# A recurrence with mixture-of-experts attention on one core: a newly searched order, 33 warming products, alternating quarters

## The chip, the cores and the metric

The kernel runs on one core of a Trainium2 chip. The time is the device time of one execution in microseconds; the number to compare is the median of several executions. Engines: TensorE (PE) multiplies matrices, VectorE (DVE) and ScalarE (ACT) work element by element and read PE's results, GpSimd (POOL) works element by element on the main on-chip memory alone, SyncE (SP) issues the loads and stores.

## What is computed

Two stages, in float32. The first is a recurrence over 768 time steps for 4 batches and 8 heads of width 48:

```python
for t in range(S):
    cur = einsum('bhd,bhe->bhde', u * k[t], v[t])
    y[t] = einsum('bhd,bhde->bhe', r[t], state + cur)
    state = w[t][:, None] * state + einsum('bhd,bhe->bhde', k[t], v[t])
```

Its output x, 4 x 768 x 384, goes into causal attention with 4 experts, of which each token uses the 2 with the largest gate:

```python
logits = x @ w_gate                       # top 2 of 4, softmax of the two
for e in range(4):
    q, k, v = x @ wq[e], x @ wk[e], x @ wv[e]         # width 64
    a = softmax(causal(q @ k.T / 8))
    out += gate[e] * (a @ v @ wo[e])
```

## The kernel before

The work is cut into 8 units: 4 batches, each in two halves of 384 steps. Every unit runs first a recurrence part, then an attention part. The recurrence part takes the 8 heads as 4 pairs; a pair's 384 steps form 6 chunks of 64. For each pair, VectorE and GpSimd build running products of the decay by scans (`w`, `suf`, lines 518 to 524), scale the streams `lt` with them (527, 529), and form `kt` (531) and `pre` (533, called `mr` in the planner). PE transposes `kt` (`ktp`), ScalarE evicts that (`kts`), PE forms the chunk states `ups` (403), and VectorE chains them chunk by chunk into `wst` (414); the first chunk of a pair is only copied (ScalarE or VectorE). `ys` is `wst` scaled (424). PE forms the products inside a chunk, `aps` (585), for two pairs together; they are masked into `am` (590) and, with `ys`, give the output `yps` (356, 358). In unit one only, the bonus term u is a small product `rk` (509) and is added to `yps` by a product with the identity (363). In the other units it is done by VectorE, GpSimd and ScalarE (538 to 561).

The attention part transposes x (`xp`, `xh`, `xl`), projects it (`pp` for q and k, `vp` for v), and runs score tiles `sp` (787), their maximum on VectorE (798), the exponential on ScalarE (803), transposes `tp` (232, or 228 as whole blocks), products with v `yp` (845), the gates, and the output projection `op` (913).

The order on every engine is written out. Each piece of work is registered with `plan.add` under a kind, with the engines that may do it and an estimated duration. A table of numbers, `ORDER`, then lists all pieces in one order, each with a letter for its engine (P, V, A, G, S) and its number; `Plan.order` walks through it, and every engine executes its pieces in that order. Numbers that the list leaves out are not executed; a transpose becomes a whole-block one where PE's last product used the whole array. Two more rules come from the last loop of the kernel: a load on SP waits for the PE piece that stands ahead of it in the list ("pace"), and some GpSimd kinds wait for the last VectorE piece of certain kinds ahead of them ("port").

Numbers 5 to 98 are 94 possible warming products: multiplications of a block of zeros (line 965) whose result nobody reads. The list before executes 14 of them.

The estimated durations that the change touches are `T_SC` and `T_SC3` (score tiles by size) and the one of `aps`. They reach the chip only through the search that made the list.

Of the kernel before, what the change touches and what calls it, by code (L numbers as in the profile page):

```python
# [1012 lines left out]
P174 V255 P166 P212 V246 A175 V256 A167 A213 S352 P185 A186 S237 P229 A230 P187 A188 V258 V214 V189 G260 V215 V190 V216
S251 V191 V217 V192 G296 V218 A209 G219 S290 G194 V257 P26 V307 A184 V247 V292 P220 V221 G311 V223 G360 A248 V193 V293
V308 V259 V294 V312 V295 V313 P1127 V309 P1131 P225 A226 P227 V298 A228 P231 A232 V261 V355 P265 V300 A267 V262 V301 P233
V310 S252 S367 A266 A234 P281 P268 V282 V275 P319 V269 G297 V276 A249 S305 A284 V270 G314 V277 V271 V278 G299 V272 V279
A263 G280 V273 P1132 V302 V103 V356 V101 V370 V357 V359 V374 S408 A321 V358 V315 A264 S473 G274 V371 S368 P1128 G316 P1129
P1070 P1066 P1067 A320 P1068 A1130 P1133 G416 A1069 A303 P1071 P1072 A1134 P322 A1073 V329 A105 G285 V323 V330 V324 S306 A317 V331
P335 P1097 V1098 G411 P1074 V325 V332 V1100 V326 V333 V336 S409 G378 G415 V327 G379 P1075 V338 P1076 A1101 P1106 P286 S291 G362
V1078 G375 A318 A1099 G334 V1079 V1107 S353 V1109 V372 A1108 A1077 P1115 V287 A380 V288 V1116 P1104 A1105 A1117 V1118 P1086 P1111 A1112  # L1020
P1080 P1087 V373 S369 A381 V376 V361 V106 V419 S423 G328 V412 V377 G420 P1088 P1081 A1119 P1082 P340 A1110 V342 A1090 P1122 A1123
P1120 P1113 V341 V1091 V1085 A1121 A1114 V363 P1102 A1103 P349 V1092 A350 S488 V364 G1093 G426 P346 S107 A347 A1089 V351 V348 V365
A1084 A1083 P400 P382 P343 P1124 P1125 P1126 G476 G430 S354 V401 A383 A384 V403 A1094 A344 V345 V427 V1095 V413 P385 A421 A386
G431 V387 A393 S474 P1135 V1138 P1144 A1165 V1145 P1195 V1136 V394 A366 V388 V389 G417 G1096 V1147 V395 P1191 P1196 V414 S424 V396
V390 G418 G432 V397 P1197 A1146 A1148 P1153 S410 P1151 V428 V391 V398 A1198 V1154 P1199 P1192 V1156 P1193 A1152 P1200 A1137 P1140 A108
P1149 A1194 A1150 S542 A1141 V429 V480 V484 G392 G399 P1222 V496 V477 A1155 V481 V434 V482 V491 G433 P1231 V478 A1157 P1205 P1201
G495 V1234 V1232 A422 V479 P1206 A1203 A1202 P1207 V1204 A1139 P438 V492 P1158 A440 A1159 V1210 A439 G485 V1167 V1223 A1233 A1235 P10
P1259 P1260 P1142 S527 A1224 V1143 G435 V1225 P456 V459 V493 P441 A449 S489 A442 V450 V457 V451 G1168 V443 A1208 A1209 A436 V444
P405 P1169 V1170 V445 G497 V452 P1261 G109 P1160 V446 V407 G549 A1262 V406 A1161 V453 G483 P1211 S425 P1212 V447 P1171 V454 V1172
V545 A437 A486 G455 A1173 S605 V494 V550 V530 P1213 V1216 G499 A1214 P1242 V1245 S544 V531 V1174 G487 G534 P503 A505 A504 A1215  # L1030
P1162 P1163 P1164 A1166 A1246 G448 S543 P1236 A1238 V1243 P1239 A1241 P1175 V1176 A1177 V532 V500 V498 V1217 V533 S590 P1263 P1264 V546
G612 A1237 G1178 G1218 A1240 P1265 P1250 A1252 A1251 A1244 A1266 V501 G598 P506 V513 S591 V507 V508 V514 V509 V547 P519 V520 A522
P461 V462 A1226 V510 V515 G593 V463 S475 V516 A502 G535 S528 V517 V511 P1187 P1267 P1229 V1270 V1268 V537 V551 A1230 V536 G512
G518 A1269 V608 P1179 V597 G523 P1180 S646 P1227 A1228 A1219 S490 A1181 P1276 V1277 P1247 A1248 V1279 A1249 V1220 A1278 V548 V594 V609
V601 G553 G599 V595 P1183 P1184 P1272 P1287 V1290 A1185 A1273 V1288 V538 V554 V596 G614 G552 P557 A1280 P1188 P1253 P467 G613 P470
V610 A559 A558 A1291 P464 A468 A465 V466 V469 P1254 A471 P1255 V472 A1289 A1189 V555 G649 P560 V561 V562 S661 V567 A556 V563
P524 V568 V569 G539 A1271 V564 G1221 P573 G653 V570 S529 G600 S592 V526 V565 V571 V574 V525 V576 G664 V1306 V669 G572 G566
V611 V602 P1335 A540 V650 V654 S606 V651 P1256 P1257 P1258 V616 A1304 P1274 A1275 V665 A541 S711 V617 P1292 V652 P620 V615 A1293
G1307 G668 V618 G714 P1284 A621 A1286 P1336 A622 V666 G655 A1294 S647 P1393 P1394 P1337 P1395 A1285 P623 A1338 V603 P578 S726 A631
A624 V625 V626 A1396 V1397 A619 V1339 V632 V627 V580 V633 G656 S648 V579 V628 V634 V635 A604 V629 V636 V667 P1281 P1330 P1308  # L1040
V1309 G637 A1283 V718 V670 A1282 V657 S712 V719 S662 G630 V729 G671 S765 P1331 P1332 P638 P584 A585 G658 P1295 A1297 A1296 A1333
V1334 V639 V586 A641 P1398 P1399 P587 A588 V589 V733 V672 V715 V730 V673 G642 P1400 P1298 P581 A582 V583 A1401 S780 S607 V674
V1402 P676 A678 A677 G722 P1363 V1364 A659 P1299 P1300 P679 A687 A680 G772 V688 V681 V689 A675 G734 V682 S727 V690 G720 A660
S1182 G735 V683 V1366 V716 G723 G783 P694 V695 P1310 V1311 A1365 V691 S766 P1301 P1302 P1303 A1305 V684 V697 P643 V645 P1314 V1315
V717 V787 S1186 V721 V692 A1316 P1481 P1368 A1369 G693 V644 G686 G768 P1482 P1483 V1485 V685 V1484 G788 A724 V1486 V731 G737 P1459
# [136 lines left out]
```

## Time and profile before

| | |
|---|---|
| median of 3 executions | 325.89 us (325.88, 330.29, 325.89) |
| the profiled execution | 329.57 us, span of its instructions 327.8 us |
| mean granted TensorE clock | 0.978 of full |
| busy: TensorE / VectorE / ScalarE / GpSimd | 311.1 / 275.6 / 237.0 / 144.3 us |

Times in the rows are in us from the first instruction of the profiled execution. A row of the timeline gives start, duration, engine, line, operation, tile written and tiles read, how many records are merged, and in brackets how long the engine stood idle ahead of it and what released it. A float32 product leaves two records. [...]

### The profile page before, as it was taken

What the parts mean: (1) busy time and instruction counts of PE and PEld (TensorE: products, weight loads), DVE (VectorE), ACT (ScalarE), POOL (GpSimd) and SP (SyncE); (2) the same over time, 40 slices, a digit from 0 to 9 for tenths busy, and PEclk for the clock granted to TensorE, in tenths of its full rate; (3) what the DMA queues carried; (4) which work ended last, traced back from release to release, by engine and by line L of the source; (5) the groups of instructions that cost most, each with busy time, mean ns of one, the idle gap of its engine ahead of it and who ended that gap; (6) DMA issues with size and microseconds to landing.
All of it is one profiled execution on the core that took longest, in us unless ns stands there. A gap on an engine that the chain in (4) does not pass through costs nothing.

```text
span 327.8 us, 13409 instructions
## 1 busy us (share of the span) xinstructions
PE 311.1 (95%) x5343; PEld 253.0 (77%) x5343; DVE 275.6 (84%) x876; ACT 237.0 (72%) x860; POOL 144.3 (44%) x277
## 2 busy tenths in 40 slices
PE   5899999999999988999799999999999999999995
PEld 2687757778877875899686987799888877978684
DVE  6897999999999998999778999989788755467852
ACT  3437799889989977687757887748868638477961
POOL 2055455668475665766447863466310100210320
PEclk9976999999999999999989999999999999999999
DMA  7989686754652975754418381441200001020012
GB/s 261 302 209 246 185 184 179 180 144 116 176 161 68 236 214 119 220 144 112 98 33 255 75 226 20 130 141 40 75 27 2 1 2 49 2 83 15 3 54 92
DMA packets 17758, 39.98 MB, mean 122 GB/s; under 512 B 2592, under 2 KB 10528, under 8 KB 17696
## 3 DMA queue, kind: packets, MB, share of 16 engines
q1 hardware_dynamic: 17696, 39.13, 43.5%
q8 instruction: 42, 0.69, 0.9%
q14 instruction: 20, 0.16, 0.2%
HBM read 34.40 MB, written 4.72 MB: 119 GB/s over the span
## 4 chain that ended last, share of the span: by engine, by line
PE 64%; DVE 21%; issue 6%; ACT 4%; DMA 3%; POOL 1%; SPq 1%; DVEq 0%; POOLq 0%; ACTq 0%
PE yp L845 10%; PE sp L787 9%; PE pp L682 9%; PE op L913 7%; PE vp L720 6%; PE tp L232 5%; PE ups L403 3%; PE yps L358 3%; DVE wst L414 3%; DVE a L798 3%; PE yps L356 2%; PE aps L585 2%; DVE w L524 2%; DMA lt<-in_wkr_dram 2%; DVE am L590 2%
## 5 line engine op out<-in xcount | busy, mean ns | idle before, releaser
L798 DVE CUSTOM_DVE_ANT_0 a<-sp,causal 128x128 f32<-128x128 f32 (+5 forms) x96 | 56.7, 618 | 19.3 <-PE sp L787 14.4
L803 ACT ACTIVATE a<-a,mx 128x128 f32<-128x128 f32 (+5 forms) x96 | 64.2, 670 | 8.9 <-DVE mx L798 8.9
L236 ACT COPY ATa<-tp 128x512 f32<-128x512 f32 (+3 forms) x75 | 35.4, 491 | 18.7 <-PE tp L232 13.6
L845 PE MATMUL yp<-ATa,v_sb 128*64 128x384 f32 (+2 forms) x240 | 36.9, 440 | 0.5 <-DVE Ql L696 0.4
L414 DVE SCALAR_TENSOR_TENSOR wst<-wst,suf,ups 112x48 f32<-112x48 f32 x160 | 34.3, 257 | 2.8 <-ACT wst L236 1.6
L682 PE MATMUL pp<-xh,wh_qk 128*128 128x384 f32 x84 | 31.3, 373 | 1.1 <-DVE Ql L696 1.0
L787 PE MATMUL sp<-K,Q 64*128 64x384 f32 (+4 forms) x160 | 31.0, 423 | 1.1 <-DVE xl L624 0.6
L559 ACT ACTIVATE xn<-nat,rk 128x48 f32<-128x48 f32 x120 | 29.0, 327 | 1.3 <-DVE rk L552 1.3
L682 PE MATMUL pp<-xh,wl_qk 128*128 128x384 f32 x84 | 28.5, 339 | 0.0
L682 PE MATMUL pp<-xl,wh_qk 128*128 128x384 f32 x84 | 28.2, 336 | 0.0
L358 PE MATMUL yps<-ys,pre 64*64 64x48 f32 (+1 forms) x704 | 25.8, 225 | 1.9 <-issue 1.7
L232 PEld LDWEIGHTS tp<-ident,a 64*128 64x128 f32 x530 | 22.0, 139 | 7.0 <-issue 1.6
L232 PE MATMUL tp<-ident,a 64*128 64x64 f32 x530 | 26.0, 228 | 0.7 <-ACT ATa L236 0.4
L356 PE MATMUL yps<-vy,am 64*64 64x48 f32 x768 | 26.3, 225 | 0.0
L845 PEld LDWEIGHTS yp<-ATa,v_sb 128*64 128x64 f32 x240 | 15.4, 139 | 14.0 <-issue 10.1
L358 PEld LDWEIGHTS yps<-ys,pre 64*64 64x64 f32 (+1 forms) x704 | 22.8, 138 | 4.0 <-issue 2.6
L533 POOL TENSOR_TENSOR pre<-lt,w 128x384 f32<-128x384 f32 x18 | 16.8, 936 | 17.6 <-DVE lt L529 5.6
L356 PEld LDWEIGHTS yps<-vy,am 64*64 64x64 f32 x768 | 23.8, 139 | 0.0
L550 ACT ACTIVATE nat<-nat 128x48 f32<-128x48 f32 x102 | 23.3, 237 | 0.3 <-POOL nat L542 0.3
L424 POOL TENSOR_TENSOR ys<-wst,suf 112x240 f32<-112x240 f32 (+1 forms) x28 | 21.7, 787 | 2.9 <-DVE wst L414 2.0
L787 PEld LDWEIGHTS sp<-K,Q 64*128 64x128 f32 x160 | 15.3, 188 | 8.4 <-issue 3.2
L902 POOL TENSOR_TENSOR yl<-yr,yh 128x384 fp32r<-128x384 f32 x9 | 9.0, 1009 | 26.8 <-ACT yh L901 26.7
(160 smaller groups left out, 927.1 us busy)
## 6 DMA issues: line engine op xcount, KB each, us to landing
lt<-in_wkr_dram SPq DMA_DIRECT2D x56, 218.6 KB, 4.1
nat<-in_nat_dram SPq DMA_DIRECT2D x28, 432.0 KB, 4.2
vy<-in_vY_dram SPq DMA_DIRECT2D x32, 144.0 KB, 3.2
out_dram<-ob SPq DMA_DIRECT2D x24, 192.0 KB, 2.0
lt<-in_wkr_dram SPq DMA_DIRECT2D x3, 583.0 KB, 6.3
w_qk<-in_wqk_dram SPq DMA_DIRECT2D x1, 768.0 KB, 8.6
nat<-in_nat_dram SPq DMA_DIRECT2D x4, 144.0 KB, 6.0
w_vg<-in_wvg_dram SPq DMA_DIRECT2D x1, 390.0 KB, 7.1
```

Source lines behind the costliest of these rows:

```text
L232: nc.tensor.transpose(o()[:, h * 512 + i * 64:h * 512 + i * 64 + 64], src[r], ident[r, r])
L236: nc.scalar.copy(o, i)
L356: nc.tensor.matmul(to, am()[k, c, :], vy()[k, c, :], start=zero and x == 0, stop=not first and i == 2 and x == len(group) - 1)
L358: nc.tensor.matmul(to, pre()[r, c, 0:C], ys()[r, c, :], start=i == x == 0, stop=False)
L414: nc.vector.scalar_tensor_tensor(new, ws[0:112, c0 + c - 1, :], sfv()[0:112, c, 0:1], upk()[0:112, o], op0=ALU.mult, op1=ALU.add)
L550: nc.scalar.activation(o, o, AF.Copy, accum_out=rk()[:, i, h:h + 1])
L559: nc.scalar.mul(xn()[:, i, (2 * p + h) * D:(2 * p + h + 1) * D], v()[:, i, h, :], rk()[:, i, h:h + 1])
L682: nc.tensor.matmul(pp()[:, 0:384], w[:, qk, k, cs], x()[:, k, :], start=(k == j == 0), stop=(k == j == 2))
L787: nc.tensor.matmul(spv(x)[:, h, :], q_()[p, t], flat(k_())[p, o], start=j == 0, stop=j == len(terms) - 1)
L798: nc.vector.tensor_tensor_reduce(out=a()[:, 0:n].rearrange("p (a n) -> p a n", a=np_), in0=spv(x), in1=causal[:, S - n:S].rearrange("p (a ...
L803: plan.add("exp", {"ACT": t_exp(n)}, lambda e, x=x, y=y, mx=mx, a=a: nc.scalar.activation(a()[:, 0:n], a()[:, 0:n], AF.Exp, bias=mx(), sca ...
L845: nc.tensor.matmul(yp()[e * 64:e * 64 + 64, lo:hi], v_sb[ep]()[:, j, e * 64:e * 64 + 64], at, start=(j == 0), stop=(j == nj - 1))
```

## The change

The order of all pieces is replaced: 2,059 entries become 2,080. Of the pieces that both lists have, 207 change their engine: VectorE loses `kt` 8 times (18 to 10), and gains `mr` (14 to 18), `rw` (16 to 19) and a few more; VectorE has 8 pieces fewer in all, ScalarE 10 more, GpSimd as many as before. 33 warming products are executed instead of 14. The two products `aps` of unit one are issued in another order: for each chunk, first both heads of one pair, then both heads of the other, so that two products that follow each other use different quarters of the array; in the other units that sequence is what it was. The estimates for score tiles rise, and the one for unit one's `aps` as well; these numbers are only read by the search.

```diff
             def amat(e, two=two, apss=apss):
                 for c in range(NH):
-                    for h in range(2):
-                        for x, (_, kt, pre, *_) in enumerate(two):
+                    for a in range(2):
+                        for z in range(2):
+                            h, x = (z, a) if first else (a, z)
+                            kt, pre = two[x][1:3]
                             nc.tensor.matmul(apss[x]()[half(h if first else h ^ x), c * C:(c + 1) * C], kt()[half(h), c, :], pre()[half(h), c, 0:C],
                                              start=True, stop=True)
-            plan.add("aps", {"PE": T_APS * (2 if first else 1)}, amat, [k for t in two for k in t[1:3]], [(apk, x) for x in range(2)], mode="Q", claim=[t[3] for t in two])
+            plan.add("aps", {"PE": 1800 if first else T_APS}, amat, [k for t in two for k in t[1:3]], [(apk, x) for x in range(2)], mode="Q", claim=[t[3] for t in two])
...
-S110 S111 V1 S3 V2 V117 V118 S136 V119 V114 V120 S113 V121 V122 S195 S138 V123 V142 V139 V124 S112 V147 P21 S170
...
+S110 V1 P32 S111 S136 V2 S3 S113 S170 P26 V117 P12 V118 V119 V114 P11 P18 V120 P9 P36 V122 P13 P21 P37
...
-T_SC = (239, 452, 666, 880, 1094, 1307)
-T_SC3 = (220, 370, 530, 690, 890, 1045)
+T_SC = (302, 515, 729, 943, 1157, 1370)
+T_SC3 = (362, 434, 603, 763, 978, 1133)
```

On PE, at the start of the program, the order before has five warming products and then unit one's first bonus product and transpose (line numbers after the change are 2 higher there):

```order
L965 MATMUL warm_170<-causal 128x512
L965 LDWEIGHTS causal
L965 MATMUL warm_181<-causal 128x512
L509 MATMUL rk_183<-u_t,nat_125 64x1 x12
L232 MATMUL ktp_200<-ident,kt_135 128x64 x6
L509 MATMUL rk_215<-u_t,nat_139 64x1 x12
```

and the changed kernel, where the first row here is the twentieth warming product:

```order
L967 MATMUL warm_200<-causal 128x512
L967 LDWEIGHTS causal
L967 MATMUL warm_202<-causal 128x512
L509 MATMUL rk_205<-u_t,nat_134 64x1 x12
L967 LDWEIGHTS causal
L967 MATMUL warm_218<-causal 128x512
...
L967 MATMUL warm_225<-causal 128x512
L228 MATMUL ktp_227<-ident,kt_174 128x128 x3
L509 MATMUL rk_242<-u_t,nat_159 64x1 x12
```

The first `rk` has moved behind 16 more warming products, four more stand between it and the transpose, and that transpose is now done in whole blocks.

On SP, the first loads before (`lt_66` in two parts is the first pair's streams, the other `lt` are the other pairs'):

```order
L245 DMA lt_66<-in_wkr_dram 128x398
L245 DMA lt_66<-in_wkr_dram 128x768
L959 DMA u_t<-in_uT_dram 128x8
L245 DMA lt_67<-in_wkr_dram 128x1166
L245 DMA vy_128<-in_vY_dram 128x288
L245 DMA lt_68<-in_wkr_dram 128x1166
L245 DMA vy_133<-in_vY_dram 128x288
L245 DMA nat_125<-in_nat_dram 128x288
L245 DMA lt_69<-in_wkr_dram 128x1166
```

and after:

```order
L245 DMA lt_66<-in_wkr_dram 128x398
L245 DMA lt_66<-in_wkr_dram 128x768
L245 DMA lt_67<-in_wkr_dram 128x1166
L961 DMA u_t<-in_uT_dram 128x8
L245 DMA vy_122<-in_vY_dram 128x288
L245 DMA lt_68<-in_wkr_dram 128x1166
L245 DMA vy_163<-in_vY_dram 128x288
L245 DMA nat_134<-in_nat_dram 128x288
L245 DMA lt_69<-in_wkr_dram 128x1166
```

The sequence is nearly the same, but the pairs behind the tiles have changed places, and in the list the second to sixth load now stand behind the first warming product, the seventh behind the 12th and the next five behind the 16th; before, the first eight stood ahead of all PE work.

On GpSimd, behind the constants, the order before:

```order
L529 TENSOR_TENSOR lt_68<-lt_68 128x192
L501 TENSOR_TENSOR nat_268<-lt_69 128x2x192
L518 TENSOR_TENSOR w_271<-lt_66 128x199
L527 TENSOR_TENSOR lt_69<-lt_69 128x192
L424 TENSOR_TENSOR ys_343<-wst_87,suf_148 112x240
```

and after:

```order
L531 TENSOR_TENSOR kt_315<-lt_69,suf_284 128x2x192
L533 TENSOR_TENSOR pre_321<-lt_68,w_182 128x2x192
L424 TENSOR_TENSOR ys_373<-wst_86,suf_131 112x240
L424 TENSOR_TENSOR ys_387<-wst_87,suf_176 112x240
L527 TENSOR_TENSOR lt_67<-lt_67 128x192
```

GpSimd now begins with a `kt` and a `pre` of unit one, both of which VectorE did before.

## Rows read from the trace of the kernel before

**Rows 1.** The page: busy us (share of the span) and records of each engine.

```profile
PE 311.1 (95%) x5343; PEld 253.0 (77%) x5343; DVE 275.6 (84%) x876; ACT 237.0 (72%) x860; POOL 144.3 (44%) x277
```

**Rows 2.** Busy time by stretch, us: length, PE, weight loads, VectorE, ScalarE, GpSimd.

```profile
core 0: us, PE busy (x) PEld busy (x) DVE busy (x) ACT busy (x) POOL busy (x), PEclk, DMA share, GB/s
0.00:20.00 20.00, 14.54 (x202) 9.83 (x206) 16.18 (x52) 7.07 (x24) 5.97 (x19) 1.00 0.91 267
20.00:31.00 11.00, 10.74 (x239) 9.74 (x240) 9.25 (x30) 6.57 (x26) 3.36 (x4) 0.54 0.92 226
31.00:45.00 14.00, 12.89 (x252) 8.59 (x250) 14.00 (x39) 11.64 (x56) 6.92 (x9) 1.00 0.80 203
45.00:140.00 95.00, 91.00 (x1903) 72.16 (x1902) 91.94 (x292) 80.26 (x322) 60.92 (x101) 1.00 0.62 165
140.00:200.00 60.00, 57.80 (x1017) 48.90 (x1019) 52.80 (x169) 45.58 (x165) 36.47 (x67) 0.97 0.49 130
200.00:328.00 128.00, 124.12 (x1742) 103.78 (x1742) 91.41 (x300) 85.84 (x273) 30.67 (x79) 1.00 0.14 46
```

**Rows 3.** Timeline of PE, 0 to 32 us.

```profile
1.42 2.31 PE L965 MATMUL warm<-causal 128*128 128x512 bf16 x5 [1.42 <-POOL causal L255]
5.64 1.44 PE L509 MATMUL rk<-u_t,nat 64*64 64x1 f32 x24 [1.91 <-DVE nat L501]
...
14.32 2.82 PE L585 MATMUL aps<-pre,kt 64*64 64x64 f32 x48
...
18.06 0.82 PE L965 MATMUL warm<-causal 128*128 128x512 bf16 x3
18.83 0.86 PE L509 MATMUL rk<-u_t,nat 64*64 64x1 f32 x24
...
27.87 2.65 PE L585 MATMUL aps<-pre,kt 64*64 64x64 f32 x48
30.44 1.56 PE L675 MATMUL pp<-xh,w_qk 128*128 128x384 f32 x4
```

**Rows 4.** Timeline of VectorE, 7 to 31 us.

```profile
7.53 0.37 DVE L518 TENSOR_TENSOR w<-lt 128x199 f32<-128x199 f32 x1 [0.47 <-DMA lt<-in_wkr_dram]
...
13.16 0.37 DVE L518 TENSOR_TENSOR w<-lt 128x199 f32<-128x199 f32 x1 [1.10 <-DMA lt<-in_wkr_dram]
...
14.19 0.54 DVE L533 TENSOR_TENSOR pre<-lt,w 128x384 f32<-128x384 f32 x1
...
19.96 0.95 DVE L533 TENSOR_TENSOR pre<-lt,w 128x384 f32<-128x384 f32 x1
...
27.71 1.49 DVE L414 SCALAR_TENSOR_TENSOR wst<-wst,suf,ups 112x48 f32<-112x48 f32 x8 [1.58 <-ACT wst L236]
...
30.55 1.02 DVE L590 TENSOR_TENSOR am<-aps,dec_mask 128x384 f32<-128x384 f32 x2 [0.17 <-PE aps L585]
```

**Rows 5.** Timeline of SP's queue: the first loads' issue.

```profile
0.74 0.85 SPq L245 DMA_DIRECT2D lt<-in_wkr_dram  x2
...
2.10 0.43 SPq L245 DMA_DIRECT2D lt<-in_wkr_dram  x1
```

**Rows 6.** Timeline of PE: an `aps` of a later unit, four quarters.

```profile
58.65 0.93 PE L585 MATMUL aps<-pre,kt 64*64 64x64 f32 x48
```

**Rows 7.** Timeline of PE at 162 us, and busy time by stretch behind it.

```profile
162.20 0.27 PE L358 MATMUL yps<-ys,pre 64*64 64x48 f32 x4 [1.69 <-issue]
...
163.00:166.00 3.00, 3.00 (x22) 1.73 (x21) 2.41 (x8) 0.34 (x2) 1.30 (x5) 0.54 0.02 5
```

**Rows 8.** Groups by line: `kt` on VectorE and on GpSimd.

```profile
L531 DVE TENSOR_TENSOR kt<-lt,suf 128x384 f32<-128x384 f32 x18 | 10.4, 590 | 0.0
L531 POOL TENSOR_TENSOR kt<-lt,suf 128x384 f32<-128x384 f32 x14 | 13.1, 939 | 7.9 <-DVE inv_pre L522 3.1 <-DVE pre L533 2.4 <-DVE w L524 1.3
```

More of the change, by code (lines that the diff above doesn't have):

```diff
@@ L1013 @@
[L1013 to L1045, printed above, removed]
@@ new lines @@
+V121 V124 P35 P5 V139 V142 S172 P33 P6 P28 P25 S112 V123 V143 V146 S195 S137 V144 V176 V173 S171 V145 S138 V148
+P7 V177 P19 P30 P24 P20 V180 P115 P22 S4 P10 P17 P15 P126 A127 V147 V181 V149 S250 V201 V178 P140 A116 P128
+P34 A0 P31 S104 V198 S235 P16 V202 V205 P151 A152 P8 A129 A141 P153 S236 V179 G207 P29 A154 V155 G183 V130 V156
+P161 P23 P27 A150 V131 V162 S99 P14 A105 V157 V132 V158 V133 G135 V159 S196 P210 V134 V182 V253 V206 G160 V254 V164
+V203 G242 V243 A125 V204 V238 V208 P185 A211 P166 S304 S197 A186 A167 P168 S289 P187 V246 A169 V239 P174 V247 A188 S290
@@ new lines @@
+V258 P229 A175 V189 V240 V190 P212 V213 A230 P220 V191 S306 G244 V214 V192 G257 V215 V193 V241 G194 V259 A184 V216 G245
+P199 V221 G296 V217 V223 S251 V255 A100 V218 V311 A248 A200 V256 V292 V307 V300 P1131 V293 P1127 G219 A209 P225 S352 V260
+V308 V294 P227 A249 V312 V297 V261 P265 V301 V262 V313 A226 V298 V355 V295 A228 A266 S367 A267 V359 V299 P231 P281 A232
+P268 V375 V269 V275 A284 V270 V302 P233 V276 S305 A234 V271 A102 G101 P1128 V277 V272 V282 V278 P1129 P1132 G285 V273 V309
+V279 A263 G274 V360 V370 V310 V371 V314 A264 G280 A303 V315 V356 V316 V357 P1066 S353 P1067 P1133 P1070 A1134 V374 V358 S252
@@ new lines @@
+P1071 P1072 A1073 P319 S237 A320 S423 A1130 A321 P1068 P1074 P1075 P322 P335 S368 V336 V329 A1069 P1097 A317 A338 V1098 V1100 P1076
+V330 G376 V323 V372 S408 V331 V324 V1079 A1099 A1077 G361 V332 P1080 V325 V326 G339 V333 V327 P1106 A1101 P286 S291 V1109 G363
+G334 A318 A1110 P1115 G328 V1107 A1078 S409 V103 P1081 P1113 V373 V378 V411 P1082 P1086 P1087 P1088 V1118 V1116 A1114 A1083 V287 V1085
+G377 V288 G364 S473 V1091 A1108 V362 V415 P1104 V379 V1092 G426 P340 A1117 A1119 V341 A1090 A1105 V342 P1102 V106 V416 S488 A1103
@@ new lines @@
+A1089 P1120 V412 V380 A1121 P1122 A1123 S107 P1111 A1112 P349 A350 V351 P382 G1093 S354 A383 P346 G431 A384 A347 P1124 V348 A365
+P400 G419 V401 P385 A393 A386 P343 V403 P1125 A1084 A1094 P1126 G480 P1135 A344 V394 A381 G476 S424 V345 V395 V1138 V1136 P1144
+V413 V396 V387 G417 V1147 V427 V414 V1095 P1153 V1145 A1137 V388 A1165 A1148 P1191 V1154 V428 A366 P1195 V389 A1146 P1192 P1140 A1141
+G481 G418 V1156 P1193 V397 P1196 V390 A1194 V398 A1155 S410 G1096 P1149 A1157 G399 P1151 P1199 P1197 A1198 V391 S369 V429 V491 A1152
@@ new lines @@
+A1150 V477 G392 V434 V420 V430 P1200 A1139 P1201 A1202 P1222 P1231 V492 A1203 V433 A421 V1204 A108 V1232 G432 S474 G495 V1234 V1167
+G482 V478 V435 V479 P1205 P1206 G1168 P1207 P1142 A1209 A1143 P1259 A1233 P1158 P438 V1223 A1159 V1210 S542 A440 G109 A439 G484 A422
+V1225 P1260 V436 P1261 G497 A1224 P456 P441 A442 S489 P405 V459 V457 A449 V443 A1208 V450 V444 A1262 V451 P1169 P1160 S527 A1235
+A1161 V1170 V407 P1211 V445 V406 A437 P1212 S543 V483 V452 P1171 P1213 V446 G485 V453 G545 V447 V454 A1215 S590 P1242 V1172 A1214
@@ new lines @@
+G499 V493 A1226 A1173 S544 S425 V1245 P1239 V1216 A1241 V1243 A1240 G1174 V530 V535 P1162 P1163 A1246 P1164 V496 A1166 V494 A486 V500
+G448 P1175 V498 V1217 P503 V531 P1236 G455 A504 V546 A1237 P1263 P1250 V549 A505 A1238 A1251 V532 V1176 P1264 P1265 P506 V501 A1252
+A1177 P519 V507 V513 G1218 V520 V514 V508 G598 P461 A1266 A522 V1178 V533 A1219 V509 S475 V515 V462 V510 V516 V511 V517 G593
+V463 G523 P1267 V1270 V1268 A502 G551 G534 V547 V553 G518 A487 V537 V550 S490 V536 S591 G597 P1179 S528 S605 G601 P1187 P1229
@@ new lines @@
+A1230 A1244 P1227 A1228 P1180 P1276 V1279 A1181 V1277 V554 S661 V1220 V548 P1188 V594 A1271 P1247 A1269 A1248 V538 V552 V539 A1249 G512
+P1183 A1280 G608 P1272 P1184 P1287 A1273 P557 G664 A1185 V1288 V1290 S646 G602 A1278 A559 A558 V595 V540 A1289 G612 G1221 P1253 V555
+P1254 G668 P467 A468 P470 A471 V469 P464 P1255 A465 V472 V466 V599 V609 P1256 A1189 A556 V596 G614 P560 V567 S606 P573 V561
+V610 V568 V574 P524 V569 V562 V570 G600 A576 S592 V563 G577 A603 V571 V525 G572 V526 P1335 V564 S529 V649 P1336 P620 A1291
@@ new lines @@
+A622 V611 S711 A621 V650 P1337 A1338 V1339 G613 V565 V1306 G616 V651 A604 P1257 P1258 P623 A631 A624 V632 A1304 V615 A541 S647
+G566 V617 V652 V665 G653 V625 V633 P1274 P1330 P1284 V626 A1286 S662 P1331 V634 P1393 S1182 P1332 P1394 A1285 G1307 A1275 A1333 P638
+V627 V635 V628 P578 G655 V1334 V636 G714 G657 P1308 G672 S648 A618 G630 V639 V629 P1395 V641 V580 V579 V1309 A619 S607 S726
+A1396 V1397 V654 P1281 A1283 A1282 P1295 A1297 A1296 V673 V670 G637 V715 P1292 G658 G669 V666 G719 A1293 P1398 P1310 V1311 A1294 P1363
@@ new lines @@
+P584 P587 A588 A585 P1399 P1314 V1366 P1400 V1364 A1312 A1367 V589 S712 V586 A1401 V667 V656 P581 A582 P676 A677 A678 V671 S780
+V583 V716 G729 A674 A659 V1402 G734 P643 P679 V680 P694 V730 A687 V733 V717 V681 V688 V731 G721 A697 G735 P1298 V689 V644
+P1299 S765 P1300 P1301 P1302 V645 S663 V695 V682 P1303 V718 V722 V732 V723 G736 A675 P1372 A1305 P1381 P1459 G720 P1460 V1315 V690
+P1481 V683 V691 S727 A660 S713 P1461 G787 P1482 V684 G698 V692 V685 G772 V1382 A1365 V1375 V1373 S766 S828 P1483 P741 A1462 A1316
@@ new lines @@
+A1485 V1463 V1484 P1368 V1486 P1529 P1469 V1384 P1530 G693 V768 V783 V788 V1313 V769 A1385 V737 A742 V770 P1470 P1531 P1471 G686 V738
+G1317 V724 P757 A1369 A743 P744 A1532 V1533 S843 A1473 V771 V745 A1374 V746 P699 A1472 G773 V1474 V751 V758 A725 A1383 G831 V752
+V753 S781 V747 V701 A739 P1475 P1534 P1476 P1477 A1478 V754 G775 A1479 P1535 G776 V700 V1480 V748 V784 V749 A1376 P1536 A1537 A760
+V785 P1464 G846 V1538 V755 V786 G756 P1370 V1487 P1465 G1488 P1466 P705 A1467 V1468 P702 P1326 S728 A706 V707 A703 P1327 V704 V740
@@ new lines @@
+V971 S965 P1672 A1673 P876 P825 V877 S901 G958 A826 P822 V879 A1563 V968 G1025 V827 A823 A1561 V824 V1674 P1523 P1524 P1525 P1526
+P1527 P1528 V1578 P1556 A1557 A1558 G1026 A1576 G973 P1553 G1579 V954 V955 A1555 S1325 G910 A1554 V969 P881 G975 V883 A898 P1564 A1566
+A1565 P1567 V970 A1568 P1455 P1736 G911 G1021 P1456 A1457 S886 V882 P1737 P1546 A1569 P1580 P1738 V1581 A1739 A1547 V912 P1582 V1583 V1740
+G974 P917 A918 A925 V919 V920 V926 V927 V921 G959 S966 G1006 V928 A1584 P932 V922 G976 S950 V923 V935 A977 V929 V930 G924
```

92 lines of the change are left out of this document (40 added, 52 removed).

## The prediction

> **What bounds the kernel now.** I read the share of busy time first, then busy time by stretch, then the waits of TensorE and VectorE in order of time. VectorE (DVE) is busy 84% of the span [rows 1], but by stretch [rows 2] the kernel has three parts. From 200 us on TensorE (PE) works 124.12 of 128 us and VectorE only 91.41: there PE's work alone sets the time. (From 140 to 200 us it works 57.80 of 60, and most of the rest is one wait, below.) From 45 to 140 us both are nearly full, PE 91.00 and VectorE 91.94 of 95 us, so either could be the limit and the slack is 4.0 us on PE and 3.1 us on VectorE. From 0 to 45 us VectorE is full from 31 on (14.00 of 14.00), and before it stands idle 3.8 us (0 to 20) and 1.75 us (20 to 31), while PE is idle 5.5 us in 0 to 20.
>
> The clock matters only at the start. The profile prints a granted clock of 1.00 for 0 to 20 us, but PE's own rows contradict it [rows 3]: the 24 records of `rk` at 5.64 us took 1.44 us, and the same 24 at 18.83 took 0.86; five warming products at 1.42 took 2.31 us (0.46 each), three at 18.06 took 0.82 (0.27 each). [...] Ahead of the first rise PE waited 1.42 and 1.91 us [rows 3]. [...]
>
> [...]
>
> **Which time the sum is made against.** The profiled execution took 329.57 us, the median run 325.89. The profiled one has one wait of 1.69 us inside `yps` at 162.20, released by nothing shown, and behind it the granted clock is 0.54 for 3 us [rows 7]; PE then loses about half of those 3 us. 1.7 + 1.5 = 3.2 us. The order of work does not ask for that wait, so a usual run is taken as 329.57 - 3.2 = 326.4 us, which is 0.5 above the median.
>
> **The change, part by part.**
>
> *Warming products*, 14 become 33, 21 of them ahead of the first `rk`. At 0.46 us each they end at 1.42 + 9.7 = 11.1 us, at 0.27 each at 7.1 us, so the first `rk` product moves from 5.64 to between 7 and 11 us. Behind it stand `ktp`, `ups`, and ScalarE's first `wst` copy, for which VectorE waits with its first `wst` step. That step has 28 VectorE instructions of unit one ahead of it before and 29 after, so it comes at the same 16 us; a PE that is 1.5 to 5.5 us late is covered by its 5.5 us of idle time. Without that cover every us would be paid. What they give: PE has no long gap ahead of 17 us, so its clock should rise early and hold. [...]
>
> *VectorE at the start.* Ahead of the second `aps` stand 13 fewer VectorE instructions (7 fewer `wst` steps, 2 fewer `kt`, `mr` and `pre` each); at the mean of a VectorE record, 275.6 / 876 = 0.31 us [rows 1], that is 4.1 us. So the second `aps` can go from 27.87 [rows 3] to about 24, and the first projection `pp` from 30.44 to about 26. But ahead of the last `yp` product of unit one's first two experts stand 6 more VectorE instructions than before (+1.9 us), ahead of the same place in unit three 2 fewer, ahead of the first `yp` of unit four 3 more (+0.9): the work is put in another order, not lowered, until PE alone is the limit. So the gain is in waits, not in work: 0 from this count, bounds -1.9 to +1.9 us. The whole order has 8 fewer instructions on VectorE, but they fall where PE is the limit.
>
> *Waits at the start.* Gone, as I read the order: 1.58 (the copy behind a slow PE), 0.17, and 1.10 (that `lt` is now issued sixth, before the pause in the loads). New: every load but the first now stands behind the first warming product. The second was issued at about 1.17 us [rows 5], now at about 2.1, and the `lt` of the second pair moves from 2.10 by 0.45 us; by the durations ahead of it VectorE asks for it 0.3 us sooner. That is 0.2 + 0.7 us. Sum: 2.85 - 0.9 = 1.95 us gained. Bounds: 0 (all waits return elsewhere) and 3.3 (all four go, none comes).
>
> *`aps` of unit one by alternating quarters.* [...] The first is hidden: VectorE fetches its result at 17.7 after other work; the second was waited for 0.17 us, already counted. So 0 more; if nothing hid it, 2 x 1.8 = 3.6 us at most.
>
> *The middle, 45 to 140 us.* The whole stretch stands in another order, and nothing in the trace says which of the 3.1 us of VectorE's idle time goes. I take a third, 1.0 us; bounds 0 and 3.1. Up to unit four PE changes between whole-array and tiled products 18 times less often, while 22 more transposes run as whole blocks instead of halves; no row prices the difference, and PE is not the only limit there, so 0.
>
> *From 200 us on.* From the first `yp` of unit four to the end both orders have 67 changes of tiling and the same products: 0.
>
> Sum: 326.4 - 1.95 - 1.0 = 323.4 us; against the median, which is 0.5 lower, **323.0 us**, 0.9% faster.
>
> **The rivals.**
>
> *PE was the true limit throughout* (0.12). Then what PE gains at the start counts whole: 30.44 - 26 = 4.4 us, and its 4.0 us of waits in the middle go too: 326.4 - 8.4 = 318.0 us. For it: PE is busy 91.00 of 95 us in the middle [rows 2]. Against it: VectorE is busy 91.94 there and would have to shed 5 us of work that the order doesn't take from it.
>
> *Nothing comes of it* (0.20). The faster start meets VectorE's full stretch from 31 us [rows 2], and the waits return in another place: 325.9 us. For it: the 6 more VectorE instructions ahead of unit one's `yp` (+1.9 us) are as large as the waits saved.
>
> *GpSimd is late with `kt`, and the kernel is slower* (0.20). `kt` goes from VectorE to GpSimd 8 times (14 become 22), two of them at the start. There it takes 0.94 us instead of 0.59 [rows 8], and `ktp`, `kts`, `ups` and all `wst` steps stand behind it. A VectorE instruction beside a GpSimd one also grows: `pre` took 0.54 us at 14.19 with GpSimd idle and 0.95 at 19.96 with `ys` running there [rows 4]. In the worst case each `kt` costs 0.35 + 0.41 us on VectorE's path: 8 x 0.76 = 6.1 us, 323.0 + 6.1 = 329.1; in the likely form of this rival 0.76 us is paid six times, 327.6 us. It decides once more than 2.9 us of it is paid. Against it: `mr` comes back from GpSimd 4 times and `rw` 3 times, so GpSimd's total hardly changes. [...]
>
> **How the numbers follow.** The forecast has 0.48, with a range of its own of 321 to 325 us (its bounds 3.3 + 3.1 us of waits and +-1.9 us of work, not all at one end). The range for 8 in 10 reaches half into both outer rivals: 318.5 to 328.0 us; it leaves out the lower part of the first and the worst form of the last. A change under 2% is about what a measurement of this kernel can tell from none: faster is below 319.4, slower above 332.4. Faster: most of the first rival, 0.11. Slower: a slower rival doubled by late loads, 0.04. Same: 0.85.
>
> **What would show it.** Right: warming products at 0.27 us or less before 10 us, `rk` at about 0.86 us for 24 records in all four places, PE's granted clock at 1.00 over 20 to 31; the first `pp` at 25 to 27 us; VectorE's wait for `wst` from ScalarE at 27 gone; VectorE's idle time over 0 to 45 down from 5.6 to about 3.7 us; the same PE work from 200 us on. Wrong: a clock that falls again before 31; VectorE waiting on GpSimd's `kt` or on a load for more than 1 us at one place; PE's idle time in 45 to 140 far from 4 us in either direction; a wait like that at 162.20 in the usual runs, not only in some.

## The result, and the profile after

The changed kernel is slightly slower than before, not faster: 328.44 us median of 12 executions (326.92 to 330.92) against 327.09 us for the kernel before, run beside it on the same chip (12 executions, 325.18 to 330.29). The ratio is 1.0059, 95% interval 1.003 to 1.0088, which is +1.9 us of 327. The forecast was a ratio of 0.991 (-2.9 us), so 4.8 us are to be explained. Ratios, here and below, leave out the executions that a slower state of the chip disturbed; medians are over all of them.

The page of the profiled execution (326.92 us, the fastest of the twelve; span 325.0), busy time by engine; it answers to [rows 1]:

```profile
PE 310.1 (95%) x5272; PEld 250.6 (77%) x5273; DVE 272.3 (84%) x865; ACT 241.8 (74%) x861; POOL 148.2 (46%) x277
```

Busy time by stretch, in the columns of [rows 2]:

```profile
0.00:20.00 20.00, 16.22 (x188) 8.80 (x189) 16.14 (x52) 4.93 (x17) 5.94 (x17) 1.00 0.87 245
20.00:31.00 11.00, 7.96 (x248) 7.77 (x248) 7.03 (x22) 6.70 (x22) 3.31 (x5) 0.69 0.82 215
31.00:45.00 14.00, 12.88 (x251) 8.81 (x250) 13.40 (x43) 13.03 (x61) 5.93 (x7) 1.00 0.67 184
45.00:140.00 95.00, 91.88 (x1840) 73.46 (x1839) 93.11 (x297) 83.90 (x336) 60.38 (x99) 1.00 0.61 162
```

The two profiled executions must not be compared by their ends: the one of before held the 1.69 us standstill at 162.20 and the low clock behind it [rows 7], and nothing of that size happened after. The changed kernel came out of the fourth `aps` 2.16 us late (the rows below: 48.12 against 45.96 us), was nearly level when two thirds of all `yps` products were done (160.6 us against 160.4), and gained its lead only past before's standstill. So it lost time at the start and won some of it back in the middle.

Timeline of PE, the fourth `aps`: before, then after.

```profile
45.96 0.88 PE L585 MATMUL aps<-pre,kt 64*64 64x64 f32 x45
```

```profile
48.12 0.88 PE L587 MATMUL aps<-pre,kt 64*64 64x64 f32 x45
```

**The start, as it went.** Timeline of PE after, to be held against [rows 3] (line numbers stand 2 higher):

```profile
1.42 7.57 PE L967 MATMUL warm<-causal 128*128 128x512 bf16 x21 [1.42 <-POOL causal L255]
8.91 0.86 PE L509 MATMUL rk<-u_t,nat 64*64 64x1 f32 x24
...
15.02 1.61 PE L587 MATMUL aps<-pre,kt 64*64 64x64 f32 x48
...
22.96 0.34 PE L358 MATMUL yps<-ys,pre 64*64 64x48 f32 x2 [3.59 <-ACT kts L236]
...
29.09 1.61 PE L587 MATMUL aps<-pre,kt 64*64 64x64 f32 x48
30.53 0.81 PE L509 MATMUL rk<-u_t,nat 64*64 64x1 f32 x24
31.28 1.56 PE L677 MATMUL pp<-xh,w_qk 128*128 128x384 f32 x4
```

Up to 18 us PE goes as forecast: the warming products end at 9 us, `rk` takes 0.86 us, `aps` 1.61 us. Then PE stands 3.59 us for ScalarE. This is what ScalarE did (timeline of ScalarE after):

```profile
20.25 0.84 ACT L316 CAST wh_vg<-w_vg 128x780 fp32r<-128x780 f32 x1 [3.35 <-DMA w_vg<-in_wvg_dram]
20.99 1.46 ACT L559 ACTIVATE xn<-vy,rk 128x48 f32<-128x48 f32 x6
22.36 0.83 ACT L236 COPY kts<-ktp 128x384 f32<-128x384 f32 x2
```

The cast of the weights `w_vg`, whose result nobody reads before 59.8 us, stands in ScalarE's queue ahead of the two `kts` copies that PE waits for, and its load had not landed. SP's queue and the duration of that load (the group's columns: issues, KB each, median us from issue to landing):

```profile
11.11 0.97 SPq L442 DMA_DIRECT2D lt<-in_wkr_dram  x2
12.82 0.35 SPq L245 DMA_DIRECT2D w_vg<-in_wvg_dram  x1
13.78 0.78 SPq L442 DMA_DIRECT2D lt<-in_wkr_dram  x2
...
17.21 0.35 SPq L245 DMA_DIRECT2D w_qk<-in_wqk_dram  x1
```

```profile
w_vg<-in_wvg_dram SPq DMA_DIRECT2D x1, 390.0 KB, 7.4
```

And the `lt` issued behind it, at 13.78 us, is the one for which VectorE stands longest (timeline of VectorE after, against [rows 4]):

```profile
13.73 0.37 DVE L518 TENSOR_TENSOR w<-lt 128x199 f32<-128x199 f32 x1 [0.71 <-DMA lt<-in_wkr_dram]
...
23.31 0.36 DVE L529 TENSOR_TENSOR lt<-lt 128x192 f32<-128x192 f32 x1 [2.02 <-DMA lt<-in_wkr_dram]
...
27.49 0.26 DVE L414 SCALAR_TENSOR_TENSOR wst<-wst,suf,ups 112x48 f32<-112x48 f32 x1 [0.79 <-ACT wst L236]
29.21 0.21 DVE L238 COPY wst<-ups 112x48 f32<-112x48 f32 x1 [1.16 <-PE ups L403]
```

With PE idle the clock fell again, as these four stretches show (PE's busy time is the second number; the granted clock, PEclk in [rows 2], the third from the end):

```profile
20.00:22.00 2.00, 0.00 (x0) 0.00 (x0) 1.28 (x3) 1.75 (x6) 0.31 (x1) 0.72 1.01 322
22.00:24.00 2.00, 1.04 (x40) 1.07 (x43) 0.69 (x2) 1.19 (x4) 0.57 (x1) 0.50 0.77 280
24.00:26.00 2.00, 2.00 (x71) 2.00 (x68) 2.00 (x5) 0.40 (x1) 0.08 (x1) 0.50 0.12 40
26.00:28.00 2.00, 2.00 (x62) 2.00 (x55) 1.21 (x6) 0.60 (x2) 1.12 (x2) 0.57 1.01 232
```

PE did nothing from 20 to 22 us, and when its work came, from 22 to 26 us, its granted clock was 0.50. So the warmth that 21 products had bought was gone where it was to be used, and the first `pp` started at 31.28 us instead of 26, even later than before's 30.44 [rows 3].

The kernel before has the same pattern, with the other weights (timeline of ScalarE before). The prediction followed the waits of PE and VectorE only:

```profile
19.30 0.83 ACT L316 CAST wh_qk<-w_qk 128x768 fp32r<-128x768 f32 x1 [3.13 <-DMA w_qk<-in_wqk_dram]
```

### The profile page after: what moved, and what is told of

It reads as the page before. It is cut to its first block, busy times and chain, and to the rows that moved or that the text cites. A ratio compares the mean times of both kernels' runs of the same rounds, so it can differ in the third digit from the quotient of the medians.

```text
span 325.0 us, 13246 instructions
## 1 busy us (share of the span) xinstructions
PE 310.1 (95%) x5272; PEld 250.6 (77%) x5273; DVE 272.3 (84%) x865; ACT 241.8 (74%) x861; POOL 148.2 (46%) x277
## 4 chain that ended last, share of the span: by engine, by line
PE 70%; DVE 16%; ACT 5%; DMA 4%; issue 3%; SPq 1%; POOL 0%; DVEq 0%; ACTq 0%; POOLq 0%
PE pp L684 11%; PE sp L789 10%; PE yp L847 10%; PE op L915 8%; PE vp L722 7%; PE tp L232 4%; DVE a L800 3%; PE warm L967 3%; PE tp L228 3%; PE yps L356 3%; PE yps L358 3%; DMA w_vg<-in_wvg_dram 2%; DVE wst L414 2%; PE ups L403 2%; DVE am L592 2%
## 5 line engine op out<-in xcount | busy, mean ns | idle before, releaser
L847 PE MATMUL yp<-ATa,v_sb 128*64 128x384 f32 (+2 forms) x240 | 35.6, 430 | 0.0
L531 POOL TENSOR_TENSOR kt<-lt,suf 128x384 f32<-128x384 f32 x22 | 20.5, 936 | 30.1 <-DVE w L524 16.5
L559 ACT ACTIVATE xn<-nat,rk 128x48 f32<-128x48 f32 x132 | 32.0, 330 | 0.7 <-DVE rk L552 0.7
L424 POOL TENSOR_TENSOR ys<-wst,suf 112x240 f32<-112x240 f32 (+1 forms) x29 | 23.8, 831 | 3.2 <-DVE wst L414 2.4
L356 PEld LDWEIGHTS yps<-vy,am 64*64 64x64 f32 x768 | 24.6, 139 | 0.7 <-issue 0.5
L550 ACT ACTIVATE nat<-nat 128x48 f32<-128x48 f32 x90 | 20.6, 240 | 2.3 <-issue 1.3
L236 ACT COPY kts<-ktp 128x384 f32<-128x384 f32 x32 | 14.2, 483 | 10.5 <-PE ktp L228 10.3
L232 PE MATMUL tp<-ident,a 64*128 64x64 f32 x436 | 21.1, 226 | 0.5 <-DVE xn L376 0.3
L232 PEld LDWEIGHTS tp<-ident,a 64*128 64x128 f32 x436 | 18.1, 138 | 4.5 <-issue 1.5
```

The costliest lines, as they stand in the source:

```text
L232: nc.tensor.transpose(o()[:, h * 512 + i * 64:h * 512 + i * 64 + 64], src[r], ident[r, r])
L236: nc.scalar.copy(o, i)
L356: nc.tensor.matmul(to, am()[k, c, :], vy()[k, c, :], start=zero and x == 0, stop=not first and i == 2 and x == len(group) - 1)
L559: nc.scalar.mul(xn()[:, i, (2 * p + h) * D:(2 * p + h + 1) * D], v()[:, i, h, :], rk()[:, i, h:h + 1])
L847: nc.tensor.matmul(yp()[e * 64:e * 64 + 64, lo:hi], v_sb[ep]()[:, j, e * 64:e * 64 + 64], at, start=(j == 0), stop=(j == nj - 1))
```

## The experiments

The theories: **A**, the cast of `w_vg` ahead of two `kts` holds PE. **B**, the loads set the start: `w_vg` on the way makes the `lt` of unit two late, and moving only the cast leaves that. **C**, the 19 more warming products cost, by themselves or because loads stand behind them. **D**, the time was lost at the start; **E**, it was lost in the middle. Every kernel is compared with the kernel before on the same chip; not all kernels ran on the same chip, so ratios are compared, not medians. Each has 12 executions, e3 and e7 six, e14 ten. Of the list `ORDER` the diffs below show only the pieces around what moves.

| kernel | what is edited | median us (before beside it) | ratio, 95% interval |
|---|---|---|---|
| changed kernel | | 328.44 (327.09) | 1.0059, 1.0030 to 1.0088 |
| e1_late_vg_cast | cast of w_vg late | 329.40 (327.37) | 1.0010, 0.9966 to 1.0055 |
| e2_late_vg_load | and its load later | 328.13 (327.37) | 0.9956, 0.9911 to 1.0001 |
| e3_14_warm | changed kernel, 14 warming products | 332.72 (327.37) | 1.0149, 1.0096 to 1.0202 |
| e5_before_alternate | before, `aps` alternating | 328.67 (327.37) | 0.9972, 0.9932 to 1.0012 |
| e6_start_of_before | changed kernel, order of before to 50 us | 326.91 (327.87) | 0.9962, 0.9925 to 0.9999 |
| e7_start_of_after | changed kernel, order of before from 50 us | 334.72 (327.87) | 1.0134, 1.0081 to 1.0187 |
| e9_before_30_warm | before, 16 more warming products | 328.55 (327.87) | 1.0043, 1.0010 to 1.0077 |
| e10_later_vg_load | e2, load of w_vg later still | 325.90 (327.87) | 0.9921, 0.9883 to 0.9959 |
| e11_nat_first | e10, one `nat` ahead of w_qk | 326.90 (326.45) | 0.9983, 0.9939 to 1.0026 |
| e12_loads_in_front | e10, loads ahead of warming | 324.94 (326.45) | 0.9957, 0.9919 to 0.9995 |
| e13_both | e11 and e12 | 325.40 (326.45) | 0.9968, 0.9931 to 1.0004 |
| e14_lt_after_aps | e12, two `lt` loads behind an `aps` | 328.85 (328.17) | 1.0039, 0.9999 to 1.0079 |

**Where was it lost: start or middle?** Both kernels are lists of the same pieces, so they can be joined: the first 340 pieces of the one (about 50 us), then what is left in the order of the other.

```diff
-ORDER = the changed kernel's list
+ORDER = the first 340 pieces of before, then the changed kernel's list without them
```

> The pieces of the order are joined: the first 340 of before (other than warming products; the four `aps` of unit one and two, six `ups` and nine `vp`, the first 50 us or so), then the rest in the order of the changed kernel. Theory D (the start lost it: the changed kernel's middle is the better one by about 2 us, since it came 2.1 us late out of the fourth `aps` at 48 us and was level with before at 160): below before, ratio 0.992 to 0.996. Theory E (the middle lost it): as the changed kernel or worse, ratio 1.004 to 1.010.

```diff
-ORDER = the changed kernel's list
+ORDER = the first 340 pieces of the changed kernel, then the list of before without them
```

> The other way round: the first 340 pieces of the changed kernel, then the rest in the order of before. Theory D (the start lost it): slower than before by the 2 us that the changed start is late at 48 us, and with no middle that gives them back, ratio 1.006 to 1.010. Theory E (the middle lost it): ratio 0.996 to 1.001.

Measured: 0.9962 and 1.0134. Theory D holds and E falls. Between the changed kernel and e6, which differ in the order of the start alone, the ratios differ by 0.97%, 3.2 us (1.6 to 4.7, an estimate from the two intervals). That is the price of the changed start. With the changed start and before's own middle (e7) the kernel is 1.3% slower than before, more than expected. With before's order at the start (e6) it beats before by 0.4% (1.2 us, interval 0 to 2.5); that is not the middle alone, since both e6 and e7 keep the changed code, with alternating `aps`. The trace of e6 shows what a start without the fall of the clock is worth (busy time by stretch, then the timeline of PE):

```profile
20.00:31.00 11.00, 8.04 (x281) 6.74 (x278) 11.00 (x34) 7.17 (x34) 3.72 (x6) 1.00 0.93 230
...
26.93 1.56 PE L677 MATMUL pp<-xh,w_qk 128*128 128x384 f32 x4
```

The clock stays at 1.00 from 20 to 31 us and VectorE is full there, with 13 warming products and before's order of work. In before's own trace it was 0.54 there [rows 2], with 14 of them and `aps` not alternating. Whether that difference decides it or each execution anew, was not tried. Over whole executions the granted clock was 0.978 to 1.000 in the 29 of before beside e6 (mean 0.987) and 0.983 to 1.000 in e6 (mean 0.993), so a part of e6's 1.2 us may be the clock.

**The cast alone.**

```diff
-P14 A105 V157
+P14 V157
...
-A321 P1068
+A321 A105 P1068
```

> The changed kernel, with one piece moved: ScalarE's cast of the projection weights w_vg (for which ScalarE stood 3.35 us at 16.9 us, with two kts evictions behind it) goes back to where the kernel before had it, after unit one's score scaling. The load itself stays. Theory A (the cast in front of kts holds PE, and the clock falls with it): the 3.6 us wait of yps for kts goes, yps starts at about 19.5 us instead of 22.96, granted clock 1.00 over 20 to 31, and the time falls by 2 to 3.5 us, to 325 to 326.5. Theory B (the lt loads set the start; VectorE waited 2.02 us for one until 23.3 us): the PE wait goes but VectorE still stands until 23.3; less than 1 us is gained, 327.5 to 328.5.

Measured: ratio 1.0010, median no lower; the interval decides neither for A nor for B. PE's wait for `kts` was gone, as A has it, and `yps` began at 18.73 us. But VectorE then stood 3.35 us for the `lt` at 23.78 and 2.19 for another at 40.97, and PE stood in `yps` itself, with nothing in the profile that released it (timeline of PE):

```profile
18.73 0.26 PE L358 MATMUL yps<-ys,pre 64*64 64x48 f32 x2
...
23.17 0.35 PE L358 MATMUL yps<-ys,pre 64*64 64x48 f32 x3 [3.75 <-issue]
```

So in this execution another standstill took the place of the first, up to the same 23 us. A names a true wait (e7, with the cast in its changed place, has it again: 3.57 us, until 22.78); what it is worth by itself these runs do not show.

**And the load.**

```diff
-P31 S104 V198
+P31 V198
...
-S304 S197
+S304 S104 S197
```

> As the run with the late cast, and the load of w_vg (390 KB) moves too, from the 15th load to the 20th, behind four streams of unit two and w_qk. Theory A: no more than the late cast alone, within 0.7 us of it. Theory B: VectorE's wait for lt at 23.3 us shrinks by 1 us or more (390 KB at 250 to 300 GB/s is 1.3 to 1.6 us), and the time falls a further 1 to 2 us below the late cast alone.

Measured: ratio 0.9956, with an interval that touches 1, and a median that does not show it. The wait for `lt` at 23 us was gone. So the load was moved further still.

```diff
-S304 S104 S197
+S304 S197
...
-S306 G244
+S306 S104 G244
```

> e2 with the load of w_vg moved further, from behind the load issued at 23.56 us to behind the one at 28.31 us (its cast stays late). Theory B (the loads of `lt` set the start): VectorE's waits for `lt` at 38.97 (1.68 us) and 42.19 (1.66 us) go, the first `pp` stays near 28.9 us, ratio 0.988 to 0.993. Rival (those waits are covered by other work, or the load of w_vg is now late for its cast): as e2, ratio 0.994 to 1.000.

Measured: 0.9921, and the median agrees; the interval lies wholly below that of the changed kernel. Both waits for `lt` were gone, the first `pp` came at 29.37 us, and the clock fell for a shorter time (0.84 over 20 to 31 us against 0.69):

```profile
20.00:31.00 11.00, 8.03 (x211) 7.07 (x213) 9.32 (x31) 6.57 (x32) 5.36 (x7) 0.84 0.83 198
```

Whole executions agree: the changed kernel's twelve were granted 0.983 to 0.994 (mean 0.989), those of e10 0.983 to 1.000 (mean 0.995), on another chip. The moves of one cast and one load, both of `w_vg`, turn the change from slower to faster, by 1.4% or 4.5 us: about the 4.8 us that were missing. How much of it is the clock, the late `lt` or PE's wait, no run separates. In the place where it was now issued, at 29.22 us, the same load took less than half as long (issues, KB, us to landing):

```profile
w_vg<-in_wvg_dram SPq DMA_DIRECT2D x1, 390.0 KB, 3.3
```

So the 7.4 us of the changed kernel go with a crowd and are not the load's own: SP issued nine other transfers between 8.3 and 14.6 us there. In the kernel before, issued at 24.05 us with seven others between 20.9 and 26.3, the same load took 7.1 us; in e10 there were two others between 24.7 and 31.0.

**The warming products.** First the changed kernel with 14 of them, as before (the first five, and nine of the twelve behind the 21st):

```diff
-V120 P9 P36 V122 P13 P21 P37 V121 V124 P35 P5
+V120 V122 V121 V124
...
```

> The changed kernel with 14 warming products instead of 33: the first 5 and nine of those behind the first rk; the rest are left out (nobody reads them). Loads that stood behind the dropped ones now stand behind the fifth. Theory A: the clock stays at its lower level until about 17 us as in the kernel before, PE at the start is slower, and the wait for w_vg remains: 0 to 1.5 us slower than the changed kernel, 328.5 to 330. Theory C (the 19 extra products and the loads that they hold back are what costs): 1 to 2 us faster than the changed kernel, 326.5 to 327.5.

Measured: 1.0149, 0.9% slower than the changed kernel. So leaving the extra warming products out costs some 2.9 us in this order, against C, and more than A expected. That this is the clock is not shown: over 20 to 31 us it was 0.84 in this trace, above the changed kernel's 0.69, and PE also waits for a load (`rk` at 7.58 us, 3.85 us for `u_t`: with fewer warming products PE asks for it before it has landed). Then the converse, 16 more in the kernel before:

```diff
-P15 P115
+P15 P6 P7 P9 P11 P12 P14 P17 P19 P22 P24 P25 P27 P29 P31 P32 P34 P115
```

> Before with 16 more warming products ahead of the first `rk` (21 there, as in the changed kernel) and nothing else. If the clock alone was worth what the forecast gave it, `rk` takes 0.86 us in all places, the clock stands at 1.00 over 20 to 31 and the first `pp` starts at 27 to 29 us instead of 30.44: ratio 0.990 to 0.996. Rival (ScalarE stands for w_qk until 19.3 us in this order as for w_vg in the changed one, so PE waits and the clock falls again): first `pp` at 30 to 31 us, ratio 0.998 to 1.003.

Measured: 1.0043, at or above what the rival expected: the warming alone gains nothing there. Timelines of ScalarE and of PE in that kernel:

```profile
20.93 0.83 ACT L316 CAST wh_qk<-w_qk 128x768 fp32r<-128x768 f32 x1 [5.53 <-DMA w_qk<-in_wqk_dram]
```

```profile
22.19 1.12 PE L509 MATMUL rk<-u_t,nat 64*64 64x1 f32 x18 [1.98 <-ACT kts L236]
...
29.80 1.56 PE L675 MATMUL pp<-xh,w_qk 128*128 128x384 f32 x4
```

`rk` took 0.86 us from 9.02 on, as forecast, but ScalarE then stood 5.53 us for w_qk instead of 3.13, PE stood for the `kts` behind that cast, and its granted clock was 0.50 from 22 to 26 us. It is the pattern of the changed kernel, made in the kernel before.

**The rest of the start.** e10's chain of work went through a `nat` that was issued at 16.75 us, right behind w_qk, and took 8.46 us; PE (timeline of e10) waited for it:

```profile
25.35 0.78 PE L403 MATMUL ups<-nat,kts 64*64 64x48 f32 x22 [2.12 <-DMA nat<-in_nat_dram]
...
29.37 1.56 PE L677 MATMUL pp<-xh,w_qk 128*128 128x384 f32 x4
```

```diff
-V162 S99 P14
+V162 P14
...
-S196 P210
+S196 S99 P210
```

> e10 with the loads of w_qk and of one `nat` exchanged (`nat` first). In e10 that `nat` was issued at 16.75, right behind w_qk, landed 8.46 us later and PE waited 2.12 us for it at 25.35. Theory B (the loads set the start): the wait falls below 0.7 us, the first `pp` moves from 29.4 to 27.5 to 28.5 us, ratio to before 0.986 to 0.991. Rival (the start is now covered, or w_qk is late in its turn): as e10, 0.991 to 0.996.

```diff
-S110 V1 P32 S111 S136 V2 S3 S113 S170
+S110 S111 S136 S3 S113 S170 S172 S112 S195 S137 S171 S138 V1 P32 V2
...
```

> e10 with the eleven loads of unit one that stand behind warming products issued ahead of the first of them (in the same order), so that none waits for PE. Theory C (holding the loads behind the warming products costs): the first `rk` or `ups` waits no longer for `nat` at 13.31 (0.97 us), the first `pp` comes 1 to 2 us earlier, ratio 0.985 to 0.990. Rival (the transfers are limited by what they move, so issuing them sooner only lets them crowd one another): as e10, 0.990 to 0.996.

> Both edits of e11 and e12 together. If both theories hold: ratio 0.980 to 0.987 and a first `pp` at 26 to 27.5 us, where the forecast had put it. If only one holds: as that one. If neither: 0.990 to 0.996.

Measured: 0.9983, 0.9957 and 0.9968. The traces did what was expected (the wait for `nat` gone in e11 and the first `pp` at 27.85; 26.59 us in e12 and in e13, where the forecast had put it), the times did not: none is faster than e10. So the rivals stand: a first `pp` earlier than e10's 29.37 us is worth nothing that these runs can measure. (e10 ran on another chip than these three, and its interval overlaps with that of each; its own 0.8% may be high.) In the traces, of the 4.7 us that e12 is ahead of the changed kernel at the first `pp`, 2.7 are left at the end, and of e13's 4.7 only 0.5. e10, e12 and, just, e6 have an interval below 1 and a median below before's: these beat the kernel before and the changed one.

**The alternating quarters.**

```diff
-                    for h in range(2):
-                        for x, (_, kt, pre, *_) in enumerate(two):
+                    for a in range(2):
+                        for z in range(2):
+                            h, x = (z, a) if first else (a, z)
+                            kt, pre = two[x][1:3]
```

> The kernel before with one edit alone: unit one's aps products alternate quarters. [...] Rival: PE sets the start, then what both products save counts: 1 to 1.5 us faster.

The prediction's own step has 0 for this. Measured, in the kernel before and nothing else changed: 0.9972, 0.9932 to 1.0012. A gain of about 2 us is not excluded, none is shown.

**The standstill inside a row of small products.** In e12 PE stood 1.04 us in the third `aps`, with nothing in the profile that released it, right behind four `lt` transfers.

```diff
-P225 S352 V260
+P225 V260
...
-S367 A267 V359 V299 P231 P281 A232
+A267 V299 P231 P281 S352 S367 V355 V359 A232
```

> e12 with the two `lt` loads of unit three that were issued at 30.5 to 33.1 us (four transfers), just ahead of the `aps` in which PE stood 1.04 us at 33.78 with nothing that the profile shows, moved behind that `aps`, together with the two VectorE pieces that read them. If that standstill comes from these transfers (PE's own instructions are brought by a queue beside them): it falls below 0.3 us, and VectorE waits 2 to 4 us for `lt` instead; ratio 0.997 to 1.005. Rival (it is not due to these transfers): a standstill of 0.7 us or more stays at the same place.

Timelines of PE in e12 and in e14, and of VectorE in e14:

```profile
33.78 0.40 PE L587 MATMUL aps<-pre,kt 64*64 64x64 f32 x13 [1.04 <-issue]
```

```profile
34.07 0.40 PE L587 MATMUL aps<-pre,kt 64*64 64x64 f32 x13 [0.98 <-issue]
...
39.80 0.37 DVE L518 TENSOR_TENSOR w<-lt 128x199 f32<-128x199 f32 x1 [3.23 <-DMA lt<-in_wkr_dram]
```

The standstill stayed, at the same product (the last 16 of 48), while VectorE now waited for `lt` and the ratio rose to 1.0039: those transfers are not its cause.

## Why the prediction was wrong, step by step

**What failed: the waits at the start, -1.95 us.** VectorE's idle time over 0 to 45 us was to fall from 5.6 to 3.7 us. By stretch it is now 45 - 16.14 - 7.03 - 13.40 = 8.4 us: up by 2.8 us instead of down by 1.95. That is 4.8 us off, as much as the whole forecast was (the agreement to a tenth is chance: e6 puts the start at 3.2 us and e7 at 4.4). Nor is VectorE's idle time a price by itself: in e10's trace it is 45 - 16.06 - 9.32 - 12.65 = 7.0 us, more than before's 5.6, and e10 is faster than before. Of the waits that were to go, which stand in brackets in [rows 4], 1.10 became 0.71 and 1.58 became 0.79 (0.39 + 0.79 = 1.2 us won); new are 2.02 for `lt`, 1.16 for `ups` (behind the PE that stood) and 0.49 for `ys`. The error was made in reading: the step priced the loads by their place in the first ten issues, followed two engines' queues, and did not ask what ScalarE's new order puts ahead of `kts`, nor when the load for it lands. With that cast and that load moved (e10) the ratio is 0.9921. Before's own list of ScalarE's waits had 3.1 us for w_qk, the pattern to look for.

**What failed with it: the clock.** That warming raises the clock by 9 us was right: `rk` took 0.86 us at 8.91, and in e9, where nothing but warming products was added, 0.86 us from 9.02 on. That a rise holds over 20 to 31 us, no row of before showed, and PE's work was not ready there: PE stood 3.59 us until 22.96, the clock was 0.69 over 20 to 31, and the first `pp` came at 31.28. "A load for more than 1 us at one place" stood in the list of signs, but no rival of its own had a place and a price for it.

**The work at the start, 0: not settled.** The second `aps` was to come at about 24 us, with 13 fewer VectorE instructions ahead of it, and came at 29.09. With the loads moved (e12, e13) the first `pp` came at 26.59 us, near the forecast's 26, but the times did not follow.

**The middle, -1.0 us: right in size, as far as shown.** VectorE's idle time over 45 to 140 us fell from 3.06 to 1.89 us; e6, which has this middle without the changed start, is 1.2 us faster than before (0 to 2.5), with alternating `aps` and more of the clock in it. In the profile the fall does not show as time, since VectorE's work in the stretch is 1.17 us more.

**`aps` by alternating quarters, 0: within what was measured**, and its duration of 1.61 us lies between the 2.65 us of [rows 3] and the 0.93 us of [rows 6]; the estimate used 1.8.

**From 200 us on, 0: right.** The lead stays as it is to the end (the last `op` product 2.8 us ahead, the last `yps` 3.1).

**The basis, 326.4 us: 0.7 too low on that chip.** The sum took the standstill at 162.20 out as an exception. It is not one: standstills of that kind lie in all 14 traces, in other places and sizes (the longest of each 0.5 to 3.8 us).

**The rivals.** GpSimd late with `kt` did not come: its 22 `kt` took what 14 did before [rows 8], and neither PE nor VectorE waited for one of them anywhere (group by tile, after: ns min/median/max):

```profile
L531 POOL TENSOR_TENSOR kt<-lt,suf x22: 924/936/952, 15.9 to 210.7; 128x384 f32<-128x384 f32 x22
```

"PE was the true limit throughout" is not borne out either: e12 and e13 have the first `pp` 4.7 us earlier than the changed kernel, and less than that is left at the end. What came was a rival that I had not named: a kernel slower because a load held the queue of an engine that PE waits for.

## What to carry to other kernels

When an order changes, list for every load its issue, its landing, its first reader, and what stands behind that reader on its engine; a reader that is in no hurry (here a cast of weights whose result is first read at 59.8 us) must not stand ahead of copies that PE waits for (3.59 us here, on ScalarE). The warm clock bought ahead was lost here (0.50 from 22 to 26 us) where PE's next work was held by such a queue: price the warming and the first wait behind it together. Two moves in a list of 2,080, of one cast and one load, decided here between a ratio of 1.006 and one of 0.992.
